# Padded score operands, zero matmuls in the prologue, a later tanh and a reordered end in a routed-attention and gated-FFN kernel

## The chip, the cores and the metric

The kernel runs on one core of a Trainium2 chip. The engines are named as the profile names them: PE (TensorE, the matmuls), PEld (its weight loads), DVE (VectorE), ACT (ScalarE), POOL (GpSimd) and SP (SyncE, which here only hands over DMAs). The metric is the device time of one execution in microseconds (us). The kernel before was run three times: 350.09 us in the median, from 348.97 to 357.59 us.

## The reference

Two blocks, one after the other. The first is attention in which a query sees only the keys of its own cluster; the second is an FFN with a convolution over the sequence (3 taps) and a gate.

```python
# attention: B=4, H=8, S=768, D=64, 16 clusters
q_assign = argmax(einsum('bhsd,hcd->bhsc', q_n, c_n))      # q, k, centroids normalised
k_assign = argmax(einsum('bhsd,hcd->bhsc', k_n, c_n))
mask   = q_assign[..., :, None] == k_assign[..., None, :]
scores = where(mask, q @ k.T / sqrt(D), -1e9)
attn   = softmax(scores);  x = attn @ v                     # heads side by side: 512 columns
# FFN: 512 -> 1024 -> 512
h    = maximum(x @ w_in, 0)
conv = sum over 3 taps of conv_w[k] * h shifted by k - 1 along S
out  = (h * sigmoid(conv)) @ w_out
```

## The kernel before, in words

**Attention.** There are 32 heads (4 batches of 8). For each head `load_qk` and `load_v` bring q, k and v in. `transposes` turns q and k (six 128x128 fp32 transposes on PE), `qkT_copy` takes them out of PSUM (DVE and ACT), `cast_qk` makes 16-bit copies on POOL and sends them by two DMAs into rows 0 to 63 of `extq` and `extk`. `assign` multiplies with the centroids (twelve fp32 matmuls of 32 columns), and `arg_a` and `arg_b` find each row's cluster (DVE and POOL) and make of it three more rows, which `bias_rows` transposes on PE (after POOL's last `pack` step) and sends by two more DMAs into rows 64 to 66. The rows make the masking part of the score matmul: 64 rows of data and 3 rows of cluster numbers give a score that is far below the others where clusters differ. `KC` is that 67.

**Slots.** The main loop has 32 slots `t`, each for two heads and one half (384) of the queries. A slot has six steps `scores(t, 0)` to `scores(t, 5)`: two matmuls (67 rows, 384 columns) into one of two PSUM buffers `sc`, then one exp on ACT. Between them the slot does, for the slot before it, `values` (attention times v, in three pairs of 12 matmuls), `normalize` (DVE: `rec`, then `x`), `x_transposes` and `xT_copy`.

**FFN units.** From slot 5 on a slot also does one unit `n = t - 5` of the FFN (256 of the 1024 hidden columns for half a sequence): `ffn_in(n, 0)` and `ffn_in(n, 1)` (four matmuls each, both into the PSUM bank `fp`), each followed by `relu` on ACT; then `taps(n, 0)` and `taps(n, 1)`, three DVE instructions each (the middle tap, L275, and the outer ones, L277). In the slot after that come `tanh` (ACT) and `gate` (DVE). In some slots `ffn_out` (eight matmuls of 512 columns into `fp`) and `evac` (a copy to SBUF and a DMA out) follow: 24 row blocks in all, `fouts` says in which slot; the ones that find no slot (`left`) are done at the end.

**Order.** Every engine works through its instructions in the order in which the program writes them; the order is written out by hand. `prepare(h, ...)` spreads the preparation of head `h` over places of the slots: three heads in slot 0, two in slot 1, one in each slot up to 25, none from 26 on. Nearly all DMAs go through SP's one queue, also in program order: loads, the two of `cast_qk`, the two of `bias_rows`, and the output. Slots 0 to 7 have no output and no or little FFN work; `half_slots_without_ffn` puts the loading of the weights there.

**Before the loop.** 24 fp32 transposes of the identity go to PE while the first loads run (L346); then heads 0, 1 and 2 are prepared in line.

**The end.** After slot 31 come unit 27 (`n` there), then units 28 to 31 (`last_in`), whose middle taps go to POOL; three whole row blocks of output; and for the last units `sigmoid`, `gate_sg` and the partial sums of the last four row blocks (`last_out`). ACT's order puts `tanh(27)` ahead of the relus of unit 28.

Of the kernel before, what the change touches and what calls it, by code (L numbers as in the profile page):

```python
# [8 lines left out]
F32 = mybir.dt.float32  # L9
# [8 lines left out]
def kernel(  # L18
# [31 lines left out]
    KC = D + 3  # L50
# [31 lines left out]
    oscale = const.tile([P, 1], F32, name="oscale")  # L82

# [82 lines left out]
    def bias_rows(h):  # L166
        pkT = where[h][1].bitcast(F16)[0 : 6 * J, 1024 - P : 1024]
        nc.tensor.transpose(pkT, pack_b[h % 3].rearrange("p a j -> p (a j)"), id16[:])  # L168
        spk = rot.tile([P, P], F16, name="spk", tag="spk")
        nc.vector.tensor_copy(out=spk[0 : 6 * J, :], in_=pkT)  # L170
        nc.sync.dma_start(extq_b[h % NE][D:KC, :], spk[0 : 3 * J, :])
        nc.sync.dma_start(extk_b[h % NE][D:KC, :], spk[3 * J : 6 * J, :])

# [6 lines left out]
    def scores(t, g):  # L180
        b, a, pr, h0 = slot(t)
        h = h0 + g // 3
        if g % 3 == 0:
            attn[t, g // 3] = rot.tile([P, J, HS], F16, name="attn", tag="attn", bufs=4)
        s = sc[nsc[0] % 2]
        nsc[0] += 1
        kt = 2 * (g % 3)
        for i in range(2):
            nc.tensor.matmul(  # L189
                s[:, i, 0:HS],  # L190
                lhsT=extk_b[h % NE][0:KC, P * (kt + i) : P * (kt + i + 1)],
                rhs=extq_b[h % NE][0:KC, HS * a : HS * (a + 1)],
                start=True,
                stop=True,
            )
        nc.scalar.activation(attn[t, g // 3][:, kt : kt + 2, :], s[:, :, 0:HS], AF.Exp, scale=0.125)  # L196
# [148 lines left out]
    for i in range(24):  # L345
        nc.tensor.transpose(sc[1][:, 0, 0:P], id128[:], id128[:])  # L346
# [22 lines left out]
    for i in range(NE):  # L369
        nc.gpsimd.memset(v16_b[i][:, :, D : D + 1], 1.0)  # L370

# [26 lines left out]
    def half_slots_without_ffn(t):  # L398
        if t == 0:
# [61 lines left out]
    for t in range(NT):  # L461
# [17 lines left out]
        if ng is not None:  # L479
            tanh(ng)  # L480
            gate(ng)
# [3 lines left out]
        if n is not None:  # L485
            if unit(n)[1]:
                carry(n)
            ffn_in(n, 0, fp)
            relu(n, 0, fp)
        run(t, 1)  # L490
        if vt is not None:
            values(vt, (2, 3))
# [22 lines left out]
        if fout:  # L515
            ffn_out(*fout, range(0, 4), fp)
        scores(t, 5)
        run(t, 5)
        if fout:
            ffn_out(*fout, range(4, NFB), fp)  # L520
            evac(*fout, fp, 0.5)
# [8 lines left out]
    ffn_in(n, 0, fp)  # L530
    relu(n, 0, fp)
# [3 lines left out]
    ffn_in(n, 1, fp)  # L535
    relu(n, 1, fp)
    carry(n)
# [5 lines left out]
    tanh(n)  # L543
    gate(n)
    left = [fouts.pop(t) for t in sorted(fouts)]
    whole = [x for x in left if x[0] < bl or x[1] < 2]

    def last_in(n):
        carry(n)
        for f, bank in enumerate((avb, fp)):  # L550
            ffn_in(n, f, bank)
            relu(n, f, bank)
            taps(n, f, nc.gpsimd)

    def last_out(u):
        for tq in range(2, J):
            ffn_out(bl, tq, (2 * u, 2 * u + 1), banks[tq - 2])
# [45 lines left out]
```

## Time and profile before

| what | value |
|---|---|
| median of 3 runs | 350.09 us (348.97 to 357.59) |
| profiled execution, time | 349.18 us |
| profiled execution, span | 347.4 us |
| mean granted PE clock | 0.919 of full |
| PE, DVE, ACT, POOL busy | 85%, 67%, 63%, 34% of the span |

The span is the time from the first instruction to the last of the profiled execution; its own device time is 1.8 us more. A row of the timeline gives the start, the time, the engine, the line, the operation and what it writes and reads, and in brackets how long the engine had been idle and whose end released it. A row of the chain of waits gives the start and the time of a piece of the path that ended last. PE is called busy while any matmul is under way, which is not the same as working at its best rate.

### The profile page before, as it was taken

To read this page: it belongs to the slowest core of one execution; us is meant where nothing else is said; L and a number is where in the kernel's file an instruction comes from. 1 tells how busy PE (TensorE), PEld (TensorE's weight loads), DVE (VectorE), ACT (ScalarE), POOL (GpSimd) and SP (SyncE) were. 2 spreads that over 40 slices of the span, in tenths; PEclk is the share of its full clock that TensorE was granted. 3 is DMA by queue.
4 is the path that set the end of the run, shared out by engine and by line. 5 is a ranking of instruction groups with operands and counts; after the bars stand their busy time and mean duration, and the time that the engine had idled before them with its cause. 6 is when DMAs were issued, how large, how long until landed. Compare 5 with 4: busy or idle time off the path is not lost.

```text
span 347.4 us, 7331 instructions
## 1 busy us (share of the span) xinstructions
PE 296.2 (85%) x2721; PEld 206.8 (60%) x2721; DVE 232.1 (67%) x512; ACT 217.8 (63%) x330; POOL 119.7 (34%) x276
## 2 busy tenths in 40 slices
PE   8799988997797998889999997899997877875863
PEld 7667767775565665566666665566664444542321
DVE  4542243437777788778888887788887776657682
ACT  4033335676677677667777786677777887862441
POOL 2254433644444233333333333333332000003460
PEclk9655557899989999999999999999999999998999
DMA  8386827673555146404444442344110000110203
GB/s 202 75 218 171 184 56 167 140 161 97 121 123 122 27 123 165 120 24 126 124 122 125 124 140 77 92 123 123 58 54 35 30 2 0 56 38 0 92 0 122
DMA packets 67194, 34.37 MB, mean 99 GB/s; under 512 B 53843, under 2 KB 64083, under 8 KB 67158
## 3 DMA queue, kind: packets, MB, share of 16 engines
q1 hardware_dynamic: 63286, 31.42, 33.1%
q0 software_dynamic: 2304, 2.10, 4.4%
q10 hardware_dynamic: 1568, 0.39, 0.5%
q8 instruction: 21, 0.34, 0.4%
q14 instruction: 15, 0.12, 0.1%
HBM read 23.11 MB, written 6.29 MB: 85 GB/s over the span
## 4 chain that ended last, share of the span: by engine, by line
DVE 41%; PE 40%; issue 8%; ACT 7%; POOL 2%; DVEq 0%; POOLq 0%; ACTq 0%
DVE cnv L277 18%; PE fp L245 10%; PE avb L203 8%; PE sc L189 6%; DVE cnv L275 6%; PE trb L134 6%; ACT attn L196 3%; DVE o_sb L326 3%; DVE eqq L148 3%; DVE x L216 3%; PE tra L110 2%; ACT th L293 2%; DVE mx L147 2%; DVE xT L230 2%; PE trb L168 2%
## 5 line engine op out<-in xcount | busy, mean ns | idle before, releaser
L196 ACT ACTIVATE attn<-sc 128x768 f16<-128x768 f32 x192 | 153.0, 809 | 82.6 <-PE sc L189 82.6
L189 PE MATMUL sc<-extq,extk 67*128 67x384 f16 x384 | 97.5, 342 | 6.9 <-ACT attn L196 6.9
L277 DVE SCALAR_TENSOR_TENSOR cnv<-hpad,cwcol,cnv 128x382 f16<-128x382 f16 (+1 forms) x128 | 80.7, 633 | 6.9 <-POOL cnv L275 2.7
L245 PE MATMUL fp<-xT,w_in 128*128 128x384 f16 x240 | 50.1, 331 | 8.6 <-DVE o_sb L326 5.1
L203 PEld LDWEIGHTS <-attn 128*128 128x128 f16 x1152 | 49.0, 100 | 8.4 <-issue 0.8
L203 PE MATMUL avb<-v,attn 128*128 128x65 f16 x1152 | 54.0, 197 | 0.0
L134 PEld LDWEIGHTS trb<-cT,qkT 128*128 128x128 f32 x360 | 50.2, 215 | 3.5 <-ACT qkT L116 1.3
L134 PE MATMUL trb<-cT,qkT 128*128 128x32 f32 x360 | 49.1, 291 | 0.1
L151 POOL TENSOR_TENSOR val<-eqq,iota_rev 128x192 f32<-128x192 f32 x30 | 17.7, 589 | 86.3 <-DVE eqq L148 86.3
L245 PEld LDWEIGHTS <-w_in 128*128 128x128 f16 x256 | 25.1, 99 | 34.2 <-issue 19.5
L189 PEld LDWEIGHTS <-extk 67*128 67x128 f16 x384 | 31.6, 103 | 20.6 <-issue 10.0
L121 POOL CAST c<-qkT 128x768 f16<-128x768 f32 x32 | 33.6, 1051 | 17.4 <-DVE qkT L115 9.4
L215 DVE RECIPROCAL rec<-avb 128x6 f32<-128x6 f32 x32 | 6.3, 196 | 45.2 <-PE avb L203 45.2
L312 PE MATMUL fp<-w_out,hg 128*128 128x512 f16 x136 | 34.9, 378 | 0.0
L312 PEld LDWEIGHTS <-hg 128*128 128x128 f16 x192 | 18.5, 98 | 25.3 <-DVE hg L308 6.3
L256 ACT ACTIVATE hpad<-fp 128x384 f16<-128x384 f32 x60 | 29.4, 490 | 5.2 <-PE fp L245 5.1
L297 DVE SCALAR_TENSOR_TENSOR hg<-th,hpad 128x764 f16<-128x764 f32 (+1 forms) x28 | 26.7, 954 | 5.8 <-ACT th L293 5.3
L293 ACT ACTIVATE th<-cnv 128x764 f32<-128x764 f16 (+1 forms) x28 | 23.6, 842 | 8.0 <-DVE cnv L277 8.0
L275 DVE TENSOR_SCALAR cnv<-hpad,cwcol 128x382 f16<-128x382 f16 (+1 forms) x56 | 23.8, 425 | 0.0
L115 DVE COPY qkT<-tra 128x512 f32<-128x512 f32 x30 | 20.5, 684 | 4.4 <-PE tra L110 4.4
L147 DVE TENSOR_REDUCE mx<-trb 128x12 f32<-128x192 f32 x30 | 10.6, 353 | 18.1 <-PE trb L134 18.1
L110 PE MATMUL tra<-id,qk_in 128*128 128x128 f32 x120 | 22.1, 315 | 0.0
(100 smaller groups left out, 286.6 us busy)
## 6 DMA issues: line engine op xcount, KB each, us to landing
qk_in<-in_q_dram SPq DMA_DIRECT2D x32, 192.0 KB
v_in<-in_v_dram SPq DMA_DIRECT2D x32, 192.0 KB
out_dram<-o_sb SPq DMA_DIRECT2D x24, 256.0 KB
qk_in<-in_k_dram SPq DMA_DIRECT2D x30, 192.0 KB
extq<-c SPq DMA_DIRECT2D x32, 96.0 KB
extk<-c SPq DMA_DIRECT2D x32, 96.0 KB
w_in<-in_moe_w_in_dram POOLq DMA_DIRECT2D x8, 128.0 KB, 4.4
w_out<-in_moe_w_out_dram POOLq DMA_DIRECT2D x8, 128.0 KB, 3.1
```

Of the source, the lines that this page charges most:

```text
L110: nc.tensor.transpose(to, qk_t[h][:, j].rearrange("p a d -> p (a d)"), id128[:])
L121: nc.gpsimd.tensor_copy(out=c[:], in_=qkT[h][:])
L134: nc.tensor.matmul(tb[:, 256 + 32 * j : 288 + 32 * j], lhsT=qkT[h][:, P * j : P * (j + 1)], rhs=cT32[:, h % H, :], start=True, stop=True,)
L189: nc.tensor.matmul(s[:, i, 0:HS], lhsT=extk_b[h % NE][0:KC, P * (kt + i) : P * (kt + i + 1)], rhs=extq_b[h % NE][0:KC, HS * a : HS * (a + 1)],
L196: nc.scalar.activation(attn[t, g // 3][:, kt : kt + 2, :], s[:, :, 0:HS], AF.Exp, scale=0.125)
L203: nc.tensor.matmul(avp[:, u, 0 : D + 1], lhsT=attn[t, hd][:, kt, P * jq : P * (jq + 1)], rhs=v16_b[(h0 + hd) % NE][:, kt, 0 : D + 1], star ...
L245: nc.tensor.matmul(bank[:, 0:HS], lhsT=w_in16[:, r, 2 * u + f, :], rhs=xT[:, b % 2, r, HS * a : HS * (a + 1)], start=(r == 0), stop=(r == ...
L256: nc.scalar.activation(hpad(n)[:, f, o : o + HS], bank[:, 0:HS], AF.Relu)
L275: (eng or nc.vector).tensor_scalar(out=cnv, in0=src, scalar1=w, scalar2=None, op0=ALU.mult)
L277: nc.vector.scalar_tensor_tensor(out=cnv, in0=src, scalar=w, in1=cnv, op0=ALU.mult, op1=ALU.add)
L293: nc.scalar.activation(th_t[n][:, :, 0:N], cnv_t.pop(n)[:, :, 0:N], AF.Tanh, scale=0.5)
L312: nc.tensor.matmul(bank[:, 0:Dm], lhsT=hg_b[b][:, fb, P * tq : P * (tq + 1)], rhs=w_out16[:, fb, :], start=(fb == 0), stop=(fb == NFB - 1) ...
```

## The change

- `extq` and `extk` are used with all 128 rows in the score matmuls. Rows 64 to 127 are set to zero once per buffer by `ext_rows`: for buffers 0 to 3 on POOL ahead of head 0, for 4 to 11 at the end of slots 0, 1 and 2, `extq` by DVE and `extk` by POOL. `bias_rows` still writes rows 64 to 66.
- `keep_busy(n)` issues `n` matmuls of a 16-bit identity with 512 columns of zeros into `sc[1]`. Twelve of them take the place of the 24 transposes; 2, 5, 6 and 6 more stand between the steps that prepare heads 0 to 2.
- In a slot, `tanh` moves from ahead of `scores(t, 1)` to behind `relu(n, 0)`, and `gate` behind the steps of place 1. The `evac` of a slot goes to ACT instead of DVE.
- Unit 27's two `ffn_in` and `relu` move into slot 31, into the bank `trb`.
- At the end the middle taps of units 28 to 31 go to ACT (a copy with a scale) instead of POOL; the banks alternate between `avb`/`fp` and `tra`/`trb`; `last_in(28)` stands ahead of `gate(27)`; the three whole row blocks get a bank each, and only one of them is evacuated on ACT.

```diff
-    KC = D + 3
+    BR = 3
+    zero = const.tile([P, 512], F16, name="zero")
 # scores
-                lhsT=extk_b[h % NE][0:KC, P * (kt + i) : P * (kt + i + 1)],
-                rhs=extq_b[h % NE][0:KC, HS * a : HS * (a + 1)],
+                lhsT=extk_b[h % NE][:, P * (kt + i) : P * (kt + i + 1)],
+                rhs=extq_b[h % NE][:, HS * a : HS * (a + 1)],
 # ahead of the loop
-    for i in range(24):
-        nc.tensor.transpose(sc[1][:, 0, 0:P], id128[:], id128[:])
+    nc.vector.memset(zero.bitcast(F32)[:], 0.0)
+    def keep_busy(n):
+        for i in range(n):
+            nc.tensor.matmul(sc[1][:, i % 2, :], lhsT=id16[:], rhs=zero[:], start=True, stop=True)
+    keep_busy(12)
...
-    for i in range(NE):
+    def ext_rows(i, eng=nc.gpsimd):
+        eng.memset(extq_b[i].bitcast(F32)[D:P, :], 0.0)
+        nc.gpsimd.memset(extk_b[i].bitcast(F32)[D:P, :], 0.0)
         nc.gpsimd.memset(v16_b[i][:, :, D : D + 1], 1.0)
+    for i in range(4):
+        ext_rows(i)
...
     cast_qk(0)
+    keep_busy(2)
     qkT_copy(1)
...
     assign(1)
+    keep_busy(5)
     bias_rows(0)
...
     transposes(2, (avb[:], fp[:]))
+    keep_busy(6)
     qkT_copy(2)
     bias_rows(1)
     assign(2)
+    keep_busy(6)
     cast_qk(2)
...
     def half_slots_without_ffn(t):
+        for i in ((4, 5, 6, 7), (8, 9), (10, 11))[t] if t < 3 else ():
+            ext_rows(i, nc.vector)
 # in a slot
         run(t, 0)
-        if ng is not None:
-            tanh(ng)
-            gate(ng)
...
             relu(n, 0, fp)
+        if ng is not None:
+            tanh(ng)
         run(t, 1)
+        if ng is not None:
+            gate(ng)
...
             x_transposes(vt)
+        if t == NT - 1:
+            ffn_in(n + 1, 0, trb)
+            relu(n + 1, 0, trb)
         scores(t, 4)
...
             ffn_out(*fout, range(0, 4), fp)
+        if t == NT - 1:
+            ffn_in(n + 1, 1, trb)
+            relu(n + 1, 1, trb)
+            carry(n + 1)
         scores(t, 5)
...
-            evac(*fout, fp, 0.5)
+            evac(*fout, fp, 0.5, on_act=True)
 # the end
+    def last_in(n):
+        carry(n)
+        for f in range(2):
+            bank = ((avb, fp), (tra, trb))[n % 2][f]
+            ffn_in(n, f, bank)
+            relu(n, f, bank)
+        for f in range(2):
+            w = cwcol[:, 2 * unit(n)[2] + f, 1:2]
+            ...
+            nc.scalar.activation(cnv_t[n][:, f, :], hpad(n)[:, f, 2 : 2 + S - CUT], AF.Copy, scale=w)
+            tap(n, f, 0)
+            tap(n, f, 2)
     tanh(n - 1)
     values(NT - 1, range(J))
     normalize(NT - 1)
-    ffn_in(n, 1, fp)
-    relu(n, 1, fp)
-    carry(n)
     gate(n - 1)
...
     taps(n, 0)
     taps(n, 1)
     tanh(n)
+    last_in(n0)
     gate(n)
-    last_in(n0)
     last_in(n0 + 1)
     for i, (b, tq) in enumerate(whole):
-        bank = (tra, trb)[i % 2]
+        bank = banks[i]
         ffn_out(b, tq, range(NFB), bank)
-        evac(b, tq, bank, 0.5, on_act=(i % 2 == 0))
+        evac(b, tq, bank, 0.5, on_act=(i == 1))
```

More of the change, by code (lines that the diff above doesn't have):

```diff
@@ L170, in bias_rows @@
         nc.vector.tensor_copy(out=spk[0 : 6 * J, :], in_=pkT)
-        nc.sync.dma_start(extq_b[h % NE][D:KC, :], spk[0 : 3 * J, :])
-        nc.sync.dma_start(extk_b[h % NE][D:KC, :], spk[3 * J : 6 * J, :])
+        nc.sync.dma_start(extq_b[h % NE][D : D + BR, :], spk[0 : 3 * J, :])
+        nc.sync.dma_start(extk_b[h % NE][D : D + BR, :], spk[3 * J : 6 * J, :])
     nsc = [0]
@@ L529, with last_out @@
     banks = [sc[0][:, 0, :], sc[0][:, 1, :], sc[1][:, 0, :], sc[1][:, 1, :]]
-    ffn_in(n, 0, fp)
-    relu(n, 0, fp)
+    left = [fouts.pop(t) for t in sorted(fouts)]
+    whole = [x for x in left if x[0] < bl or x[1] < 2]
+    def last_in(n):
[6 more added lines that the diff above has]
+            w = cwcol[:, 2 * unit(n)[2] + f, 1:2]
+            if n not in cnv_t:
+                cnv_t[n] = rot.tile([P, 2, S - CUT], F16, name="cnv", tag="cnv")
+            nc.scalar.activation(cnv_t[n][:, f, :], hpad(n)[:, f, 2 : 2 + S - CUT], AF.Copy, scale=w)
+            tap(n, f, 0)
+            tap(n, f, 2)
+    def last_out(u):
+        for tq in range(2, J):
+            ffn_out(bl, tq, (2 * u, 2 * u + 1), banks[tq - 2])
     tanh(n - 1)
@@ L543 @@
     tanh(n)
+    last_in(n0)
     gate(n)
[L545 to L557, printed above, removed]
-    last_in(n0)
     last_in(n0 + 1)
     for i, (b, tq) in enumerate(whole):
-        bank = (tra, trb)[i % 2]
+        bank = banks[i]
         ffn_out(b, tq, range(NFB), bank)
-        evac(b, tq, bank, 0.5, on_act=(i % 2 == 0))
+        evac(b, tq, bank, 0.5, on_act=(i == 1))
     for u in range(NPR):
```

## The prediction

> **What bounds the kernel now.** I read the page first, for the clock granted to PE over the span; then the engines' busy time in stretches; then the timeline of the first 75 us; then the chain of waits and the timeline of single slots; last the end. The page's row of PE's clock (40 slices of 8.7 us) has a hole of some 40 us:
>
> ```profile
> PEclk9655557899989999999999999999999999998999
> ```
>
> Asked in fine steps, the clock changes only at times that lie a multiple of 3.41 us apart, so I cut the busy table on that grid. Columns: stretch, length, busy us (instructions) of PE, PEld, DVE, ACT, POOL, then clock, DMA share, GB/s.
>
> ```profile
> 42.15:45.56 3.41, 3.41 (x25) 3.04 (x25) 1.96 (x6) 0.81 (x1) 0.84 (x3) 0.50 0.67 153
> 52.39:55.81 3.42, 3.28 (x29) 2.77 (x30) 0.91 (x2) 0.56 (x2) 2.16 (x5) 0.50 0.57 86
> ...
> 62.64:66.05 3.41, 3.41 (x42) 2.87 (x39) 1.73 (x5) 2.51 (x4) 1.61 (x3) 1.00 0.72 134
> 66.05:69.46 3.41, 3.41 (x23) 2.39 (x22) 1.13 (x3) 1.86 (x4) 2.63 (x7) 0.50 0.61 149
> 83.12:86.53 3.41, 1.88 (x22) 1.07 (x20) 2.26 (x5) 2.04 (x4) 2.59 (x6) 1.00 0.16 56
> ```
>
> PE was busy for all of 62.64 to 66.05 and lost the clock at its end; in 83.12 to 86.53 it was busy for 1.88 of 3.41 us and kept it; in 42.15 to 45.56 it was wholly busy and did not get it back. So it isn't busy time that holds the clock. The large groups of matmuls in the stretch that lost it (first two rows) and in the one that kept it (next two), and four score matmuls in the chain of waits:
>
> ```profile
> L189 PE MATMUL sc<-extq,extk 67*128 67x384 f16 x7 | 1.8, 343 | 0.0
> L134 PE MATMUL trb<-cT,qkT 128*128 128x32 f32 x12 | 1.4, 269 | 0.0
> ...
> L245 PE MATMUL fp<-xT,w_in 128*128 128x384 f16 x6 | 1.3, 325 | 0.0
> L189 PE MATMUL sc<-extq,extk 67*128 67x384 f16 x3 | 0.8, 324 | 0.0
> ...
> 64.76 0.65 PE sc L189 x4
> ```
>
> Four score matmuls in a row take 0.65 us, so 384 columns stream for 0.16 us. These matmuls stream 7 x 0.16 = 1.1 us in the losing stretch and 9 x 0.16 = 1.4 us in the keeping one; weighted by used rows (67 of 128 for scores) it is 0.6 against 1.2 us. I take it that the share of the array that streams is what counts; two stretches make that likely, not certain.
>
> **Up to slot 5.** The first score matmuls of slots 0 to 5, and three other rows of that time:
>
> ```profile
> 17.25 0.83 PE L189 MATMUL sc<-extq,extk 67*128 67x384 f16 x2
> ...
> 34.54 0.83 PE L189 MATMUL sc<-extq,extk 67*128 67x384 f16 x2
> ...
> 50.71 0.80 PE L189 MATMUL sc<-extq,extk 67*128 67x384 f16 x2
> ...
> 59.80 0.48 PE L189 MATMUL sc<-extq,extk 67*128 67x384 f16 x2 [0.57 <-ACT attn L196]
> ...
> 65.98 0.77 PE L189 MATMUL sc<-extq,extk 67*128 67x384 f16 x2
> ...
> 73.73 0.49 PE L189 MATMUL sc<-extq,extk 67*128 67x384 f16 x2 [0.57 <-ACT attn L196]
> ```
>
> ```profile
> 16.67 0.53 SPq L122 DMA_DIRECT2D extq<-c  x1
> ...
> 23.56 0.91 PEld L110 LDWEIGHTS tra<-id,qk_in 128*128 128x128 f32 x4 [0.23 <-DMA qk_in<-in_k_dram]
> ...
> 30.35 0.75 SPq L172 DMA_DIRECT2D extk<-spk  x1
> ```
>
> Slots 0 to 4 take 17.3, 16.2, 9.1, 6.2 and 7.8 us. Slots 0 and 1 run at half clock and prepare three and two heads; slots 2 and 4 run at half in part; slot 3 is wholly at full clock.
>
> Slot 0 can't shrink by half. From 16.67 to 31.1 us SP hands over 20 DMAs one right behind another (first and last shown), and the change removes none. The last are the cluster rows of head 2, with which slot 1 starts, so it can't start before about 32. PE also has to wait for head 4's keys, which come at 23.5, with slot 0 half done; that wait may well cost the clock for a stretch or two. I put slot 1 at 33 instead of 34.5: gain 1.5.
>
> Slot 1 is PE work throughout, 16.2 us at half clock, so 8 at full; 10 with waits for `pack`, and 11.5 with a stretch or two at half: gain 4.7. The padding decides here: it makes two score steps and one head's transposes stream about as much as the 52.39 stretch did, at whose end the clock came back. Slot 2 takes 6.7, slot 3's 6.2 and some memsets: gain 2.4. In slot 4 the dip of the 66.05 row goes: gain 1.5. Sum 10.1.
>
> What this costs:
>
> ```profile
> 323.59 1.47 PE trb L312 x7
> ...
> L341 DVE MEMSET cT<- 128x256 f32 x1 | 0.3, 272 | 0.9 <-PEq L587 0.9
> ...
> 7.36 0.82 POOL L121 CAST c<-qkT 128x768 f16<-128x768 f32 x1 [4.86 <-DVE qkT L115]
> ```
>
> A matmul of 512 columns streams 1.47 / 7 = 0.21 us, 0.42 at half clock. The first twelve cost 2.5 to 5 us beside loads that are awaited anyway. The other 19 cost 4.0 us; I let them delay slot 0 by nothing, since `assign(2)` runs in half its time and the rest lies in PE's waits for `pack`. Were the clock at half all the same, they would be 8.1, and some 4 would stick out. A memset of 64x384 is an estimated 0.4 us (256 columns took 0.27 on DVE; no row shows this fill on POOL, where I allow 0.2 to 1). Eight on POOL are 3.4 us, inside the 4.86 for which it idles ahead of its first cast. Those at the ends of slots 0 to 2 put 1 us on the path. The 61 more rows cost PE nothing: with 67 rows and with 128 a matmul of 384 columns shows 324 and 325 ns above. So up to slot 5 the gain is 9 us, between 2 (clock as before) and 13.
>
> [...]
>
> **The slots from 5 on.** Behind a slot with output (chain of waits, then two rows of the timeline, then two groups of the page):
>
> ```profile
> 159.97 0.21 DVE rec L215
> ...
> 165.31 0.61 DVE o_sb L326
> ...
> 165.96 0.81 PE fp L245 x4
> ...
> 168.81 0.21 DVE rec L215
> ```
>
> ```profile
> 165.27 0.49 PE L189 MATMUL sc<-extq,extk 67*128 67x384 f16 x2
> ...
> 166.00 0.21 POOL L164 TENSOR_TENSOR pack<-pack,kscale 128x12 f16<-128x12 f16 x1
> ```
>
> ```profile
> L256 ACT ACTIVATE hpad<-fp 128x384 f16<-128x384 f32 x60 | 29.4, 490 | 5.2 <-PE fp L245 5.1
> L297 DVE SCALAR_TENSOR_TENSOR hg<-th,hpad 128x764 f16<-128x764 f32 (+1 forms) x28 | 26.7, 954 | 5.8 <-ACT th L293 5.3
> ```
>
> The period is 168.81 - 159.97 = 8.84. PE has one hole: two score matmuls from 165.27 stream until 165.60, and `ffn_in` starts at 165.96, when DVE has emptied `fp`. With the copy on ACT, right behind the last `ffn_out`, this 0.36 goes, and PE alone would make 8.48. Late next is a loop: from `rec` to the end of DVE's preparation steps 5.34 (159.97 to 165.31), POOL's `pack` 0.9 (to 166.21), and bias rows to `rec` 2.04 (166.77 to 168.81): 8.3. And the gate now stands in front of `rec`: `ffn_in` 0.81, relu 0.49, tanh 0.85 and gate 0.95 end 3.1 us behind the start of `ffn_in`, the values 2.85 (168.81 - 165.96). It sticks out by 0.25, of which PE's slack takes half. Period 8.6, gain 0.24 in each of 13 slots (those behind slots 9, 10, 13 to 18, 21 to 25): 3.1.
>
> Behind a slot without output:
>
> ```profile
> 137.84 0.85 ACT th L293
> ...
> 147.05 0.85 ACT th L293
> ```
>
> ```profile
> 138.84 0.91 POOL L164 TENSOR_TENSOR pack<-pack,kscale 128x12 f16<-128x12 f16 x1
> ```
>
> The period is 9.21. Tanh waits for the last tap and holds up an exp and a relu; the gate behind it then runs beside POOL's `pack`, which takes 0.91 instead of 0.21. With both later that 0.7 goes and 8.5 is left: gain 0.7 in 8 slots (behind 5 to 8, 11, 12, 19, 20), 5.6.
>
> From slot 27 on no head is prepared, and the wait behind tanh is plain:
>
> ```profile
> 281.34 0.81 PE L245 MATMUL fp<-xT,w_in 128*128 128x384 f16 x4 [1.19 <-ACT hpad L256]
> ```
>
> These 1.19 us go; the wait for `x` and the gate in front of `rec` take half of it back: 0.55 in five slots, 2.8. Together 11.5, between 1 (the gate's 0.95 all ahead of `rec`) and 14.
>
> **The end.**
>
> ```profile
> 318.83 1.44 PE L245 MATMUL avb<-xT,w_in 128*128 128x384 f16 x4 [3.41 <-ACT hpad L256]
> ...
> 330.37 2.49 POOL L275 TENSOR_SCALAR cnv<-hpad,cwcol 128x386 f16<-128x386 f16 x2 [4.86 <-issue]
> ```
>
> Unit 27's eight matmuls in slot 31 spare the last values a wait for `fp`; I count 0.75. A unit's two middle taps took POOL 2.49; two ACT copies are 2 x 0.49 (the relu's row; no row has a copy of this shape), so 1.5 less for each unit that waits for them, three of the four: 4.5. Against that `gate(27)` now stands behind taps that wait for ACT's tanh, two relus and a copy, 0.85 + 3 x 0.49 = 2.3, with 1.6 on the path, as PE waited there before too (3.41). Gain 3.5 (0 to 5).
>
> **The rivals.**
> 1. Rows and zeros don't count, and the clock stays as it was. For it: PE's long busy stretches at half clock had score matmuls in them as well. Against: the groups above. The prologue gains 2 instead of 9, or loses 2 if the 19 zero matmuls run at half: 333 to 338.
> 2. The gate takes the place of the tanh: it stands whole in front of `rec`, and the slots gain nothing. For it: DVE is in the loop in every slot. Against: by the sum above only 0.25 of its 0.95 sticks out. 337; with the first, 345.
> 3. Slower: ACT becomes the bound of the slots. Per slot with output it has 6 exps, 2 relus, tanh, part of `qkT` and now the evacuation; if 0.85 (tanh) in 27 slots came ahead of exps that PE awaits and nothing else got shorter, 23 us less the 12.5 of prologue and end, 360. It decides from where ACT has under 0.85 us of idling left in a slot. Against: ACT waited for PE ahead of its exps for 82.6 us in all:
>
> ```profile
> L196 ACT ACTIVATE attn<-sc 128x768 f16<-128x768 f32 x192 | 153.0, 809 | 82.6 <-PE sc L189 82.6
> ```
>
> **How the numbers follow.** The profiled execution took 349.18 us (span 347.4). Less 9, 11.5 and 3.5 it is 325.2; the median of the runs stands 0.9 above it: 326. Forecast 0.62; rival 1 alone 0.17; rival 2 alone 0.12; both 0.05; rival 3 0.04. The forecast's own range is 317 to 335 (prologue 13 or 4, slots 14 or 8, end 5 or 2). To hold 8 in 10 it takes in rivals 1 and 2 as well: 316 to 340. A change of 2%, 7 us, is about what can be told from none here: below 343 lie the forecast and the first two, 0.88 with something off for sums that are wrong together; within 2% 0.08; slower 0.04.
>
> **What would show it.** The clock row: full through 11 to 21 us, a dip where PE waits for head 4's keys, full again by 40 at the latest; no dip near 66 and 100. Slot 1 starts at 32 to 34, slot 5 at 62 to 68. The periods fall to about 8.6 and 8.5; PE's wait for `fp` is gone, POOL's `pack` is at 0.21 in all slots. DVE's wait ahead of `rec` is near nil, with the gate right before it. In the last 30 us POOL has no taps. I am wrong if the clock stays at half in slot 1, if the period stays over 8.8, or if slot 0 starts later than 18.5.

## The result, and the profile after

The changed kernel takes 336.35 us in the median of 4 runs (335.39 to 337.16); its time is 0.962 of the kernel before (95% interval 0.958 to 0.966). The forecast was 326 us with a range of 316 to 340: faster, as forecast, but between the profiled executions only 13.2 us of the 24 came. Disturbed executions are left out of all comparisons here; the profile of one experiment (67 rows) is of a disturbed execution, so only its times are used. The profiled execution took 335.94 us, its span is 334.2 us.

The page's row of PE's clock, of the changed kernel (40 slices of 8.35 us):

```profile
PEclk9985876999999999999999999999999999997699
```

The dips that the kernel before had near 66 and 100 us are gone. Two things are not as forecast: between 22 and 56 us the clock is at 0.50 in three stretches (22.2 to 32.5, 39.3 to 46.1 and 49.5 to 56.4), and again for 10 us near the end (305.5 to 315.8). The starts of slots 0 to 5 and 31 in the timeline show what this cost:

```profile
17.94 0.49 PE L190 MATMUL sc<-extq,extk 128*128 128x384 f16 x2
...
33.79 0.49 PE L190 MATMUL sc<-extq,extk 128*128 128x384 f16 x2
...
48.69 0.48 PE L190 MATMUL sc<-extq,extk 128*128 128x384 f16 x2
...
58.96 0.32 PE L190 MATMUL sc<-extq,extk 128*128 128x384 f16 x1 [0.57 <-ACT attn L197]
...
71.29 0.48 PE L190 MATMUL sc<-extq,extk 128*128 128x384 f16 x2 [0.57 <-DMA qk_in<-in_k_dram]
...
286.77 0.49 PE L190 MATMUL sc<-extq,extk 128*128 128x384 f16 x2
```

| part | before, us | after, us | gain | forecast |
|---|---|---|---|---|
| up to the start of slot 5 | 73.7 | 71.3 | 2.4 | 9 (2 to 13) |
| from slot 5 to the start of slot 31 | 227.5 | 215.5 | 12.0 | 11.5 (1 to 14) |
| from there to the end of the span | 46.2 | 47.4 | -1.2 | 3.5 (0 to 5) |

**The slots came out.** Two neighbouring slots with output in the changed kernel, from the timeline:

```profile
161.33 0.19 DVE L216 RECIPROCAL rec<-avb 128x6 f32<-128x6 f32 x1
...
165.38 0.60 ACT L325 ACTIVATE o_sb<-fp 128x512 f32<-128x512 f32 x1
...
166.86 0.81 PE L246 MATMUL fp<-xT,w_in 128*128 128x384 f16 x4
167.36 0.21 POOL L165 TENSOR_TENSOR pack<-pack,kscale 128x12 f16<-128x12 f16 x1
...
169.02 0.95 DVE L298 SCALAR_TENSOR_TENSOR hg<-th,hpad 128x764 f16<-128x764 f32 x1 [0.92 <-ACT th L294]
...
169.89 0.19 DVE L216 RECIPROCAL rec<-avb 128x6 f32<-128x6 f32 x1
```

From `rec` to `rec` it is 8.56 (forecast 8.6). `ffn_in` no longer waits for `fp`, `pack` takes 0.21, and the gate stands right before `rec`, which then waits for nothing: each as forecast. DVE's wait has moved ahead of the gate, 0.92 us for tanh.

**Slot 1 did not.** DVE in slot 1 of the changed kernel, and three stretches on the clock's grid (columns as in the prediction):

```profile
35.51 0.35 DVE L160 TENSOR_REDUCE m_t<-val 128x12 f32<-128x192 f32 x1 [0.70 <-POOL val L152]
36.00 1.60 DVE L377 MEMSET extq<- 64x384 f32 x4
37.63 0.22 DVE L171 COPY spk<-trb 36x128 f16<-36x128 f16 x1
```

```profile
29.04:32.45 3.41, 3.14 (x14) 1.72 (x13) 1.98 (x5) 1.19 (x2) 1.25 (x4) 0.50 0.71 199
...
35.87:39.28 3.41, 1.39 (x21) 1.27 (x21) 2.48 (x7) 1.08 (x2) 2.69 (x10) 1.00 0.80 196
39.28:42.69 3.41, 3.41 (x26) 3.14 (x24) 0.42 (x2) 0.92 (x2) 3.08 (x14) 0.50 0.94 218
```

The clock came back at 32.45, ahead of slot 1. Then four memsets of `extq` held DVE for 1.6 us; the copy `spk` stood behind them and PE's next bias rows behind `spk`. PE was busy for 1.39 of 3.41 us, and the clock was gone again for 6.83 us.

**The end got longer.** DVE, PE and ACT behind the loop of the changed kernel:

```profile
304.23 2.46 DVE L278 SCALAR_TENSOR_TENSOR cnv<-hpad,cwcol,cnv 128x386 f16<-128x386 f16 x4 [2.23 <-ACT cnv L569]
306.61 0.94 DVE L298 SCALAR_TENSOR_TENSOR hg<-th,hpad 128x764 f16<-128x764 f32 x1
...
309.85 0.69 DVE L327 TENSOR_SCALAR o_sb<-sc 128x512 f32<-128x512 f32 x1
...
310.59 6.15 PE L313 MATMUL sc<-w_out,hg 128*128 128x512 f16 x16 [7.61 <-DVE o_sb L327]
...
314.19 0.60 ACT L325 ACTIVATE o_sb<-sc 128x512 f32<-128x512 f32 x1 [7.73 <-PE sc L313]
```

PE does the first whole row block, then waits 7.61 us for DVE's copy of it: the copy stands behind the taps of units 28 and 29 and the gate, and the second block's bank lies in the same PSUM tile. In this wait the clock falls to 0.50, and the next 16 matmuls take 6.15 us (3.62 at full clock in the combined kernel below). ACT's copy of the second block, and behind it the first `sigmoid`, wait for those.

### The profile page after: what moved, and what is told of

It reads as the page before. It is cut to its first block, busy times and chain, and to the rows that moved or that the text cites. A ratio compares the mean times of both kernels' runs of the same rounds, so it can differ in the third digit from the quotient of the medians.

```text
span 334.2 us, 7350 instructions
## 1 busy us (share of the span) xinstructions
PE 286.8 (86%) x2728; PEld 197.6 (59%) x2728; DVE 226.3 (68%) x505; ACT 227.6 (68%) x354; POOL 105.8 (32%) x284
## 4 chain that ended last, share of the span: by engine, by line
PE 57%; DVE 22%; ACT 9%; issue 4%; DMA 3%; POOL 2%; SPq 2%; POOLq 0%; DVEq 0%; ACTq 0%
PE sc L190 12%; PE trb L135 8%; PE fp L313 8%; PE avb L204 8%; DVE cnv L278 7%; PE fp L246 6%; ACT attn L197 4%; PE tra L111 4%; PE sc L313 3%; DVE hg L298 3%; DMA qk_in<-in_k_dram 3%; DVE x L217 3%; ACT th L294 2%; DVE cnv L276 2%; PE sc L350 2%
## 5 line engine op out<-in xcount | busy, mean ns | idle before, releaser
L190 PE MATMUL sc<-extq,extk 128*128 128x384 f16 x384 | 94.4, 334 | 6.9 <-ACT attn L197 6.3
L278 DVE SCALAR_TENSOR_TENSOR cnv<-hpad,cwcol,cnv 128x382 f16<-128x382 f16 (+1 forms) x128 | 78.9, 619 | 7.9 <-ACT cnv L569 3.6
L204 PEld LDWEIGHTS <-attn 128*128 128x128 f16 x1152 | 48.2, 99 | 8.8 <-issue 1.4
L135 PEld LDWEIGHTS trb<-cT,qkT 128*128 128x128 f32 x360 | 46.7, 202 | 3.8 <-ACT qkT L117 1.9
L135 PE MATMUL trb<-cT,qkT 128*128 128x32 f32 x360 | 45.7, 279 | 0.2 <-DVE qkT L116 0.2
L246 PE MATMUL fp<-xT,w_in 128*128 128x384 f16 x224 | 45.5, 326 | 0.3
L190 PEld LDWEIGHTS <-extk 128*128 128x128 f16 x384 | 30.7, 100 | 21.0 <-issue 10.4
L152 POOL TENSOR_TENSOR val<-eqq,iota_rev 128x192 f32<-128x192 f32 x30 | 17.7, 590 | 77.7 <-DVE eqq L149 77.7
L246 PEld LDWEIGHTS <-w_in 128*128 128x128 f16 x256 | 24.8, 97 | 18.3 <-issue 1.9
L313 PE MATMUL fp<-w_out,hg 128*128 128x512 f16 x136 | 34.9, 379 | 0.0
L122 POOL CAST c<-qkT 128x768 f16<-128x768 f32 x32 | 26.9, 841 | 10.0 <-DVE spk L171 5.2
L257 ACT ACTIVATE hpad<-fp 128x384 f16<-128x384 f32 x56 | 27.7, 495 | 0.2 <-PE fp L246 0.2
L313 PE MATMUL sc<-w_out,hg 128*128 128x512 f16 x56 | 15.5, 434 | 9.8 <-DVE o_sb L327 7.6
L127 POOL CAST v<-v_in 128x384 f16<-128x384 f32 x32 | 20.6, 645 | 1.5 <-DMA v_in<-in_v_dram 1.5
```

The costliest lines, as they stand in the source:

```text
L135: nc.tensor.matmul(tb[:, 256 + 32 * j : 288 + 32 * j], lhsT=qkT[h][:, P * j : P * (j + 1)], rhs=cT32[:, h % H, :], start=True, stop=True,)
L190: nc.tensor.matmul(s[:, i, 0:HS], lhsT=extk_b[h % NE][:, P * (kt + i) : P * (kt + i + 1)], rhs=extq_b[h % NE][:, HS * a : HS * (a + 1)], s ...
L204: nc.tensor.matmul(avp[:, u, 0 : D + 1], lhsT=attn[t, hd][:, kt, P * jq : P * (jq + 1)], rhs=v16_b[(h0 + hd) % NE][:, kt, 0 : D + 1], star ...
L246: nc.tensor.matmul(bank[:, 0:HS], lhsT=w_in16[:, r, 2 * u + f, :], rhs=xT[:, b % 2, r, HS * a : HS * (a + 1)], start=(r == 0), stop=(r == ...
L257: nc.scalar.activation(hpad(n)[:, f, o : o + HS], bank[:, 0:HS], AF.Relu)
L278: nc.vector.scalar_tensor_tensor(out=cnv, in0=src, scalar=w, in1=cnv, op0=ALU.mult, op1=ALU.add)
```

## The experiments

The theory after the result: (a) the padding lets PE keep its clock, as forecast, but the memsets on DVE in slot 1 (and perhaps the matmuls on zeros) give most of it back; (b) the slots' gain comes from the later tanh and from the evacuation on ACT as forecast; (c) the new end loses by its order and its banks. The rivals stand with each run. All stages come from one profiled execution per kernel; times are medians, for two kernels the values themselves. Each ratio is to the kernel before as it was run beside that kernel. Kernels with the same slots differ by up to 0.7 us in the part from slot 5 to slot 31 (215.5 to 216.2).

| kernel | time | ratio to before (95%) | slot 0 | slot 5 | 5 to 31 | 31 to end |
|---|---|---|---|---|---|---|
| before | 350.09 | 1 | 17.3 | 73.7 | 227.5 | 46.2 |
| changed | 336.35 | 0.962 (0.958, 0.966) | 17.9 | 71.3 | 215.5 | 47.4 |
| slots' edits alone | 336.5 and 338.7 | 0.963 (0.955, 0.971) | 17.6 | 74.2 | 216.7 | 43.8 |
| 67 rows | 342.1 to 345.2 | 0.977 (0.970, 0.985) | | | | |
| memsets early | 334.85 | 0.955 (0.950, 0.960) | 18.1 | 69.5 | 216.1 | 46.9 |
| other banks | 336.13 | 0.958 (0.952, 0.964) | 19.0 | 73.8 | 216.1 | 45.1 |
| old end | 336.37 | 0.960 (0.956, 0.965) | 18.3 | 72.7 | 216.1 | 45.5 |
| no zeros in line | 337.1 | 0.964 (0.958, 0.969) | 18.2 | 72.3 | 215.6 | 47.4 |
| more zeros | 334.68 | 0.955 (0.947, 0.963) | 19.0 | 71.7 | 216.2 | 46.7 |
| gate first | 335.61 | 0.959 (0.953, 0.965) | 18.8 | 73.7 | 215.6 | 46.6 |
| combined | 330.93 | 0.944 (0.938, 0.950) | 20.2 | 68.2 | 216.2 | 44.2 |
| padding alone | 343.84 | 0.981 (0.973, 0.989) | 17.7 | 65.8 | 227.4 | 47.1 |
| evacuation on DVE | 341.05 | 0.978 (0.967, 0.989) | 17.9 | 69.0 | 221.6 | 47.2 |
| tanh at its old place | 345.61 | 0.985 (0.978, 0.992) | 18.6 | 70.4 | 226.1 | 47.2 |

### The slots: each edit alone

The kernel before with the slots' edits and nothing else:

```diff
         run(t, 0)
-        if ng is not None:
-            tanh(ng)
-            gate(ng)
...
             relu(n, 0, fp)
+        if ng is not None:
+            tanh(ng)
         run(t, 1)
+        if ng is not None:
+            gate(ng)
...
-            evac(*fout, fp, 0.5)
+            evac(*fout, fp, 0.5, on_act=True)
```

> The kernel before with the three edits inside a slot alone: tanh behind relu(n, 0), gate behind place 1, the slot's evacuation on ACT. My theory: these edits alone make the gain that the changed kernel shows between slot 5 and slot 31 (227.5 us before, 215.5 after), so 12 us, about 338 us in all, with the slots up to 5 and the end as before (73.7 us to the start of slot 5; 46 us from the start of slot 31). Rival: part of those 12 us comes from the padded scores (more rows, a steadier clock); then slots 5 to 31 come out at 218 us or more and the time at 340.5 or more.

Measured: 216.7 us from slot 5 to slot 31 instead of 227.5, so these edits alone bring 10.8 of the 12.0. The dips of the clock near 67 and 91 us stayed; this kernel's score matmuls still use 67 rows. The profiled executions of this kernel and of the whole change are 0.5 us apart in span: what the rest of the change gains and loses beside the slots' edits nearly cancels.

Each of the two undone in the changed kernel:

```diff
-            evac(*fout, fp, 0.5, on_act=True)
+            evac(*fout, fp, 0.5)
```

> The changed kernel with the evacuation in the slots back on DVE. Theory, as forecast: it is worth 0.24 to 0.36 us in each slot with output, by the wait of PE for fp; periods behind such slots 8.75 to 8.85, the others 8.5 as in the changed kernel; from slot 5 to 31 218.5 to 220 instead of 215.5; time 339 to 341. Rival: the later tanh and gate bring all of it, and PE's wait for fp is covered; 215.5 to 216 and 336.5.

```diff
         run(t, 0)
+        if ng is not None:
+            tanh(ng)
+            gate(ng)
...
-        if ng is not None:
-            tanh(ng)
         run(t, 1)
-        if ng is not None:
-            gate(ng)
```

> The changed kernel with tanh and gate back at their old place, ahead of the slot's first values; the evacuation stays on ACT. Theory, as forecast: the later tanh and gate are worth 0.7 us in each slot without output and 0.55 in each of the last five slots, and little in the slots with output; periods 9.2 and 8.6, from slot 5 to 31 222 to 224 instead of 215.5, time 342.5 to 344.5. Rival 1: with the evacuation gone from DVE the old place costs little; 217 to 219, time 338 to 340. Rival 2: the old place costs in every slot, because ACT now has tanh and evacuation ahead of exps; 226 or more, time 347.

From slot 5 to slot 31 it takes:

| | tanh at its old place | tanh later |
|---|---|---|
| evacuation on DVE | 227.4 | 221.6 |
| evacuation on ACT | 226.1 | 215.5 |

Alone the evacuation is worth 1.3 us and the later tanh 5.8; together 11.9. The starts of slots 15 and 16 with what lies between them; first with the evacuation on DVE, with the wait ahead of `ffn_in` in the second row, then with tanh at its old place, with the gate and POOL's cast beside it:

```profile
155.53 0.33 PE L190 MATMUL sc<-extq,extk 128*128 128x384 f16 x1
...
157.72 0.81 PE L246 MATMUL fp<-xT,w_in 128*128 128x384 f16 x4 [0.34 <-DVE o_sb L327]
...
164.49 0.33 PE L190 MATMUL sc<-extq,extk 128*128 128x384 f16 x1
```

```profile
160.33 0.33 PE L190 MATMUL sc<-extq,extk 128*128 128x384 f16 x1
...
162.86 1.36 DVE L298 SCALAR_TENSOR_TENSOR hg<-th,hpad 128x764 f16<-128x764 f32 x1 [0.53 <-ACT th L294]
...
163.36 1.23 POOL L127 CAST v<-v_in 128x384 f16<-128x384 f32 x1
163.40 0.51 ACT L257 ACTIVATE hpad<-fp 128x384 f16<-128x384 f32 x1
163.96 0.81 PE L246 MATMUL fp<-xT,w_in 128*128 128x384 f16 x4 [0.17 <-ACT hpad L257]
...
169.11 0.33 PE L190 MATMUL sc<-extq,extk 128*128 128x384 f16 x1
```

The periods are 8.96 and 8.78, against 8.84 with neither edit and 8.55 with both. With the later tanh alone, a slot with output even gets longer than before: the gate ahead of `rec` delays what follows on DVE, the evacuation stands at the end of that, and PE waits 0.34 us for `fp`. With the evacuation on ACT alone, tanh still pushes the relu back and PE waits for that. That both waits have to go before either edit pays in full is how I read these rows; no run removes one wait by itself. The theory for the evacuation (218.5 to 220) was low, and for tanh the second rival's number came (226), though not for its reason: PE's scores wait no longer for ACT's exps than in the changed kernel (6.3 us in both pages), and the gain of each edit hangs on the other.

### The first slots: rows, memsets, zeros

The changed kernel with the score matmuls back at 67 rows; the memsets stay:

```diff
-                lhsT=extk_b[h % NE][:, P * (kt + i) : P * (kt + i + 1)],
-                rhs=extq_b[h % NE][:, HS * a : HS * (a + 1)],
+                lhsT=extk_b[h % NE][0 : D + BR, P * (kt + i) : P * (kt + i + 1)],
+                rhs=extq_b[h % NE][0 : D + BR, HS * a : HS * (a + 1)],
```

> The changed kernel with 67 instead of 128 rows in the score matmuls; the memsets, the zero matmuls and the rest stay. Theory that the clock follows the streamed share weighted by rows: PE loses the clock again near 66 and 100 us and gets it back later in slots 1 and 2, so slot 5 starts 2 to 4 us later (73 to 75 instead of 71.3) and the time is 338.5 to 341. Rival, rows don't count: the clock row and the start of slot 5 stay within 0.7 us of the changed kernel, and so does the time (336.4).

It loses 6 to 9 us, more than either expected. The granted clock over the span is 0.914 to 0.921 in these runs, against 0.947 to 0.955 in those of the changed kernel. The rival that rows don't count falls.

The memsets of buffers 4 to 7 go to POOL behind `cast_v(0)`, those of 8 to 11 to POOL alone:

```diff
     cast_v(0)
+    for i in (4, 5, 6, 7):
+        ext_rows(i)
...
-        for i in ((4, 5, 6, 7), (8, 9), (10, 11))[t] if t < 3 else ():
-            ext_rows(i, nc.vector)
+        for i in ((), (8, 9), (10, 11))[t] if t < 3 else ():
+            ext_rows(i)
```

> The changed kernel with the zero rows of buffers 4 to 7 written on POOL ahead of the loop, behind cast_v(0), where POOL idles for 5.2 us, and those of 8 to 11 on POOL alone instead of DVE and POOL. Theory: the memsets in DVE's queue at the end of slot 0 make PE wait 2.0 us for the bias rows of head 5, and that idle stretch costs the clock for the next two windows (39.3 to 46.1). Without them PE keeps the clock in slot 1, and slot 2 starts 4 to 6 us earlier (43 to 45 instead of 48.7); time 330 to 333. Rival, SP's queue and the loads set slots 1 and 2 anyway: slot 2 starts within 1.5 us of 48.7 and the time stays above 335.

The median is 1.5 us lower, less than the theory, and the ranges of the two kernels overlap (333.59 to 335.77, and 335.39 to 337.16). DVE's memsets are gone from slot 1, but in this execution the clock had not come back at slot 1's start; it stayed at half from 22.4 to 46.3 us. So this run doesn't show what the memsets cost when the clock is back. The next one comes nearer to it: the kernel before with only the rows padded and the memsets for them, at these early places on POOL.

```diff
-                lhsT=extk_b[h % NE][0:KC, P * (kt + i) : P * (kt + i + 1)],
-                rhs=extq_b[h % NE][0:KC, HS * a : HS * (a + 1)],
+                lhsT=extk_b[h % NE][:, P * (kt + i) : P * (kt + i + 1)],
+                rhs=extq_b[h % NE][:, HS * a : HS * (a + 1)],
...
+    for i in range(4):
+        ext_rows(i)
...
     cast_v(0)
+    for i in (4, 5, 6, 7):
+        ext_rows(i)
```

> The kernel before with nothing but the score operands at 128 rows and the memsets for them (all on POOL, buffers 4 to 7 early); the 24 transposes, the order of the slots and the end stay. Theory: the rows act on the clock alone; the first stretch at half ends near 46 instead of 56, the dips near 66 and 100 are gone, slot 5 starts at 71 to 72.5 instead of 73.7, the slots from 5 to 31 take 226 to 227.5 as before, and the time is 346 to 348.5. Rival 1: the rows do nothing by themselves; clock and time as before, 349 to 351. Rival 2: the run with 67 rows in the changed kernel lost 6 to 9 us, so the rows are worth that much here too: 341 to 344.

Slot 5 comes at 65.8, earlier than any theory had it, and the time, 343.84, is the second rival's. The page's clock row, the starts of slots 1, 2 and 5, and three stretches on the grid, all of this kernel:

```profile
PEclk9755999999999999999999999999999999996999
```

```profile
33.97 0.33 PE L189 MATMUL sc<-extq,extk 128*128 128x384 f16 x1
...
45.87 0.32 PE L189 MATMUL sc<-extq,extk 128*128 128x384 f16 x1
...
65.82 0.48 PE L189 MATMUL sc<-extq,extk 128*128 128x384 f16 x2 [0.57 <-ACT attn L196]
```

```profile
29.22:32.63 3.41, 3.14 (x14) 1.72 (x13) 1.98 (x5) 1.20 (x2) 1.26 (x5) 0.50 0.41 127
...
36.04:39.46 3.42, 2.41 (x29) 1.99 (x28) 1.03 (x4) 1.80 (x3) 2.94 (x14) 1.00 0.88 216
...
46.28:49.70 3.42, 2.08 (x35) 1.79 (x35) 1.26 (x3) 1.42 (x3) 2.65 (x8) 1.00 0.27 65
```

Slot 1 starts as in the changed kernel (33.97 and 33.79), with the clock back at 32.63 and 32.45: a pair alike up to there. PE's wait ahead of the second bias rows in slot 1, first in the changed kernel, then in this one:

```profile
37.90 0.21 PE L169 MATMUL trb<-id,pack 128*36 128x128 f16 x1 [2.02 <-DVE spk L171]
```

```profile
37.08 0.23 PE L168 MATMUL trb<-id,pack 128*36 128x128 f16 x1 [1.01 <-POOL oscale L410]
```

Without memsets on DVE slot 1 then takes 11.90 us instead of 14.90, the clock stays, and slot 5 comes 5.5 us sooner. This is one execution of each, and the pair differs in the matmuls on zeros as well, so the 5.5 is not a price that the memsets have everywhere. The six profiled kernels with the changed kernel's code up to slot 5 start that slot at 69.0 to 73.8; with the early memsets beside the same zeros it is 69.5, and 68.2 in the combined kernel below. In that one, without memsets on DVE, PE waited 1.29 us for a DMA of bias rows at the start of slot 1, and the clock went at 34.9 all the same.

It is also the plainest evidence for the rows: beside the memsets only they differ from the kernel before, whose clock came back at 55.8 and went twice more before 309; here it comes at 32.6 and stays to 309, through stretches in which PE is busy for 2.08 and 2.41 of 3.41 us. The slots behind slot 5 are unchanged (227.4), and a score matmul there shows the same time with 67 and with 128 rows. The groups of the score matmuls from 150 to 200 us, of the kernel before and of this one:

```profile
L189 PE MATMUL sc<-extq,extk 67*128 67x384 f16 x69 | 17.0, 325 | 0.0
```

```profile
L189 PE MATMUL sc<-extq,extk 128*128 128x384 f16 x70 | 16.9, 325 | 0.6 <-ACT attn L196 0.6
```

The changed kernel without the 19 matmuls on zeros between the first heads' steps (the first 12 stay):

```diff
-    keep_busy(2)
-    keep_busy(5)
-    keep_busy(6)
-    keep_busy(6)
```

> The changed kernel without the 19 matmuls on zeros that stand between the first heads' steps (the first 12 on zeros, ahead of the centroids' transpose, stay). Theory: they hold the clock at full from 11 to 22 us and buy little else, because the clock falls at 22 in any case; without them the clock falls at 12, slot 0 starts at 17.9 or a little later (18.5), slot 1 at 34 to 35, and the time is 336 to 338. Rival 1: they cost PE more than they give; slot 0 starts 0.7 earlier, at 17.2, and the time is 335 or less. Rival 2: they carry the whole gain of the first slots; slot 5 comes at 73.5 as in the kernel before, and the time is 338.5.

As the theory had it: the clock falls at 13.1 us (and comes back at 26.7), and the time is 337.1, too near the 336.35 to call it a difference. The 19 matmuls hold the clock for some 9 us more and buy nothing that shows.

The changed kernel with early memsets and 38 more matmuls on zeros in PE's waits:

```diff
+    def fill(cnt):
+        for i in range(cnt):
+            nc.tensor.matmul(fp[:], lhsT=id16[:], rhs=zero[:], start=True, stop=True)
+    for t, place, cnt in ((0, 2, 8), (0, 4, 6), (1, 0, 8), (1, 2, 4), (1, 5, 4), (2, 0, 8)):
+        at(t, place, lambda cnt=cnt: fill(cnt))
```

> The changed kernel with the memsets of buffers 4 to 7 early on POOL (as in the run of that name) and 38 more matmuls on zeros, in slot 0 ahead of head 4's transposes (8) and head 5's (6), in slot 1 at its start (8), in its third (4) and last part (4), and at the start of slot 2 (8), all into fp, which nothing reads then. Theory: PE's waits in slots 0 and 1 let the clock fall and the clock sets their length; with the waits filled the clock stays full from 5 to 60, slot 1 starts at 32.5 to 33.5 (SP's queue sets that) and takes 11 to 12 instead of 14.9, slot 5 starts at 65 to 67 instead of 71.3, and the time is 330 to 332. Rival: the slots are set by loads and by the chains through POOL and DVE to the bias rows, not by the clock; the clock is full, but slot 5 starts at 69 to 71 and the time is 334 to 336. A third way: the zeros stand in PE's queue ahead of needed matmuls and slot 5 comes later than 71.3.

The time is that of the run with early memsets alone (334.7 and 334.9), as the first rival had it, but slot 5 comes at 71.7, as the third way had it. Slots 1 and 2 and the wait in slot 0, from its timeline:

```profile
26.16 0.66 PE L111 MATMUL tra<-id,qk_in 128*128 128x128 f32 x4 [1.63 <-DMA qk_in<-in_k_dram]
...
37.10 0.49 PE L190 MATMUL sc<-extq,extk 128*128 128x384 f16 x2
...
51.24 0.68 PE L190 MATMUL sc<-extq,extk 128*128 128x384 f16 x2
```

The clock was at full in slot 1 (from 34.6 to 48.2), and slot 1 still took 14.1 us. The fills in it cost PE 1.89, 1.03 and 1.91 us of its own queue (the last at half clock); it seems that they took what the clock gave. Slot 0 was not helped: head 4's keys came 1.63 us after the eight fills ended.

### The end

The changed kernel with the whole end of the kernel before (unit 27 behind the loop, middle taps on POOL, banks `tra` and `trb`):

```diff
-        if t == NT - 1:
-            ffn_in(n + 1, 0, trb)
-            relu(n + 1, 0, trb)
...
-            nc.scalar.activation(cnv_t[n][:, f, :], hpad(n)[:, f, 2 : 2 + S - CUT], AF.Copy, scale=w)
-            tap(n, f, 0)
-            tap(n, f, 2)
+            taps(n, f, nc.gpsimd)
...
-        bank = banks[i]
+        bank = (tra, trb)[i % 2]
```

> The changed kernel with the end of the kernel before (unit 27's first matmuls behind the loop, the middle taps of units 28 to 31 on POOL, whole output blocks in the banks of tra and trb, gate of unit 27 ahead of unit 28). Theory: the new end is a loss of its own; from the start of slot 31 to the end the changed kernel takes 47.4 us, and the kernel before with nothing but the slots' edits 43.8, so this kernel should take 43.8 there: slot 31 at 286.8 as in the changed kernel, span 330.6, time 332.3, ratio 0.950. Rival: the 43.8 was the luck of where the clock fell in one profiled execution; then the end takes 46 to 47.5 and the time is 335 to 336.5.

The theory's 3.6 us fell: the end takes 45.5 and the time is 336.37, that of the changed kernel. The same old end takes 43.8, 46.2, 45.5 and 47.1 us in the four kernels of the table that have it, with 0, 3.4, 3.4 and 6.8 us of half clock in its middle; so the lowest of them goes with a clock that was not lost there. The new end takes 46.6 to 47.4 in seven kernels that have it as it is or with the gate moved, always with 6.8 or 10.2 us of half clock. Its loss is about 1.5 us on the profiles, and no difference in the times shows it. This run puts all edits of the end back at once, so it doesn't tell them apart.

The whole row blocks in banks of two tiles in turn:

```diff
-        bank = banks[i]
+        bank = (banks[0], banks[2], banks[1])[i]
```

> The changed kernel with one edit at the end: the second whole row block goes into the first half of sc[1] and the third into the second half of sc[0], instead of the other way round. Theory: the second block waited for the evacuation of the first (to 310.6) only because both lie in the tile sc[0]; in another tile it starts when gate(27) ends, at about 307.6, and the clock comes back 3.4 us earlier: 3 to 4.5 us less, 332 to 333.5. Rival, it waited for something else that ends then, such as the taps of unit 29 in front of it on DVE: it still starts at 310.6, and the time stays within 0.7 us.

PE then runs straight on to the block that needs unit 27:

```profile
304.18 3.19 PE L313 MATMUL sc<-w_out,hg 128*128 128x512 f16 x14
...
309.70 0.95 DVE L298 SCALAR_TENSOR_TENSOR hg<-th,hpad 128x764 f16<-128x764 f32 x1
...
310.70 0.70 PE L313 MATMUL sc<-w_out,hg 128*128 128x512 f16 x2 [3.34 <-DVE hg L298]
```

and waits for its gate. The end takes 45.1 instead of 47.4. The median of the times (336.13) is no lower; in the profiled execution slot 5 came 2.5 us later, and the other executions have no profile. The gate of unit 27 ahead of the taps of unit 28:

```diff
     tanh(n)
-    last_in(n0)
     gate(n)
+    last_in(n0)
```

> The changed kernel with the gate of unit 27 ahead of the taps of unit 28 on DVE, as before the change. Theory: in the changed kernel that gate stands behind four taps that wait 2.23 us for ACT's middle taps, and the last blocks wait for it; moved ahead, it ends about 3 us sooner, and the end from slot 31's start takes 45 to 46 instead of 47.4: time 334.5 to 335. Rival: the order doesn't matter, because the second matrix product of the output blocks waits for its bank until the first one is evacuated (7.61 us of waiting were put down to that); the end stays at 47 to 47.5 and the time at 336.

Here the gate is early, and the wait for the first block's copy stays:

```profile
306.71 4.84 DVE L278 SCALAR_TENSOR_TENSOR cnv<-hpad,cwcol,cnv 128x386 f16<-128x386 f16 x8 [0.31 <-ACT cnv L569]
...
311.46 0.69 DVE L327 TENSOR_SCALAR o_sb<-sc 128x512 f32<-128x512 f32 x1
...
312.20 6.23 PE L313 MATMUL sc<-w_out,hg 128*128 128x512 f16 x16 [6.74 <-DVE o_sb L327]
```

The end takes 46.6, a gain of 0.8. Each of the two uncovers the other's wait, so the last run has both, with the early memsets:

```diff
     cast_v(0)
+    for i in (4, 5, 6, 7):
+        ext_rows(i)
...
-        for i in ((4, 5, 6, 7), (8, 9), (10, 11))[t] if t < 3 else ():
-            ext_rows(i, nc.vector)
+        for i in ((), (8, 9), (10, 11))[t] if t < 3 else ():
+            ext_rows(i)
...
-        bank = banks[i]
+        bank = (banks[0], banks[2], banks[1])[i]
...
-    last_in(n0)
     gate(n)
+    last_in(n0)
```

> The changed kernel with three things together: the memsets of buffers 4 to 11 on POOL (4 to 7 early), the whole output blocks in banks of two different tiles in turn, and the gate of unit 27 ahead of the taps of unit 28. Theory: at the end PE first waits for the evacuation of the first block, which stands on DVE behind taps, since the second block's bank is in the same tile, and with other banks it waits for the gate of unit 27; each of the two alone uncovers the other, so both together gain more than the 2.3 and 0.8 us that they gained alone: from slot 31's start 43 to 44 instead of 47.4, with no or one stretch at half clock near 305 to 318. With slot 5 at 69.5 to 71 and 216 from there to slot 31 the time is 330 to 333. Rival: what is late at the end is the chain of units 28 to 31 on ACT and DVE; the end stays at 45 and the time at 333 to 335.

```profile
298.63 3.62 PE L313 MATMUL sc<-w_out,hg 128*128 128x512 f16 x16
...
300.50 0.95 DVE L298 SCALAR_TENSOR_TENSOR hg<-th,hpad 128x764 f16<-128x764 f32 x1 [0.97 <-ACT th L294]
...
307.26 3.57 PE L313 MATMUL sc<-w_out,hg 128*128 128x512 f16 x8 [5.02 <-DVE o_sb L327]
```

The first two blocks now run straight on, 16 matmuls in 3.62 us at full clock. The third still waits 5.02 us for a copy that stands behind taps on DVE, in which the clock goes, for 6.8 us. The end takes 44.2, so 3.2 less than 47.4. That is about the sum of the 2.3 and 0.8 alone; that both together gain more, as the theory had it, isn't shown. The time is 330.93 (330.11 to 331.73), and this kernel beats the one before and the changed one.

## Why the prediction was right, and where it failed

**The slots (11.5 forecast, 12.0 measured).** Right in sum and in its marks. The terms were mis-sized: the 13 slots with output gained 4.9 us in all and not 3.1, those without 4.1 and not 5.6, the last five 3.0 (2.8). The step "the gate now stands in front of `rec`" was right. What the gate costs there by itself isn't measured: with the evacuation left on DVE the period is 8.96, 0.12 longer than with neither edit, and with both edits it is 8.55, near the 8.48 that PE alone was said to make. Rival 2 falls, as the gate's place costs nothing that shows with both edits in. Rival 3 falls too: the scores of the changed kernel wait no longer for ACT's exps than before (6.3 and 6.9 us), as its page shows:

```profile
L190 PE MATMUL sc<-extq,extk 128*128 128x384 f16 x384 | 94.4, 334 | 6.9 <-ACT attn L197 6.3
```

**The first slots (9 forecast, 2.4 measured).** That the rows move the clock was right. Padding alone brings slot 1 to 34.0 and makes it 11.9 us long (33 and 11.5 forecast), without dips near 66 and 100, and slot 5 falls into the 62 to 68 named; the gain is 7.9. The step that failed is "those at the ends of slots 0 to 2 put 1 us on the path". The four memsets cost DVE 1.60, near the estimated 0.4 each; but they stand ahead of `spk` when PE has nothing else, PE's wait there is 2.02 instead of 1.01 us, and in the matched pair the clock went with it: 3.0 us in slot 1 and 5.5 up to slot 5. A price was put on the memsets' length and none on the clock that hangs on them. How much of the missing 6.6 us they explain stays open, since moving them in the changed kernel itself brought 1.5. "I am wrong if the clock stays at half in slot 1": it was so for half of it. Of the zeros, the claim that they delay slot 0 by nothing was not far off (17.9 for 17.3, and 18.2 without those in line), but they were counted as a help, and no run shows them to be one. Whether they are the reason that slot 5 comes at 68 to 70 with early memsets and zeros, and at 65.8 with early memsets alone, stays open: the grid's position differed between those executions too (a point of it lies at 32.63 us with the padding alone, at 32.69 with the memsets early and at 34.9 in the combined kernel).

**Rival 1** (rows don't count) falls by two runs: 67 rows cost 6 to 9 us, padding alone gives 343.84. PE's busy time by itself doesn't tell the stretches apart either: with the padding alone the clock stayed behind those with 2.41 and 2.08 of 3.41 us busy, and in the changed kernel it was gone behind two with more, as its grid shows:

```profile
18.80:22.21 3.41, 2.62 (x20) 1.76 (x18) 1.54 (x4) 1.88 (x4) 1.66 (x5) 1.00 0.84 223
22.21:25.63 3.42, 1.20 (x6) 1.21 (x7) 0.49 (x3) 0.40 (x1) 1.92 (x6) 0.50 0.89 223
...
46.11:49.52 3.41, 2.48 (x18) 1.61 (x17) 1.30 (x5) 1.93 (x3) 1.18 (x3) 1.00 0.24 58
49.52:52.93 3.41, 2.42 (x20) 2.19 (x21) 1.67 (x4) 0.88 (x2) 2.89 (x10) 0.50 0.31 71
```

The share that streams, which the prediction took from two stretches, was the author's estimate. The runs show that the rows count; what share the clock needs was not shown.

**The end (3.5 forecast, -1.2 measured, outside its own bounds).** Two steps failed. "1.5 less for each unit that waits", 4.5 in all, was too large. DVE's outer taps of the last units waited 2.7 us in all for POOL's middle taps before, and 3.6 us for ACT's in the changed kernel, as the groups by form show:

```profile
L277 DVE SCALAR_TENSOR_TENSOR cnv<-hpad,cwcol,cnv 128x386 f16<-128x386 f16 x64 | 41.2, 649 | 4.7 <-POOL cnv L275 2.7
```

```profile
L278 DVE SCALAR_TENSOR_TENSOR cnv<-hpad,cwcol,cnv 128x386 f16<-128x386 f16 x64 | 39.4, 621 | 5.6 <-ACT cnv L569 3.6
```

No run moves the middle taps alone. And the sum left out an edit of the diff: the whole blocks moved into banks of `sc` and the first copy from ACT to DVE. That copy stands behind eight taps, and the wait of 7.61 us comes from there. It isn't all of the lost clock: with other banks the half clock there still lasts 6.8 us instead of 10.2. The wait of the gate behind ACT-fed taps was seen (1.6), and alone it is worth 0.8.

## What to carry to other kernels

Where an engine's granted clock falls in its waits, as PE's fell to 0.50 here behind a stretch with 1.39 of 3.41 us busy, price a delay also by the clock that the waiting engine can lose, and not by its length alone: in the one matched pair here, 1.6 us of memsets in a queue went with 5.5 us. Fixed work such as memsets belongs where the engine waits anyway. Matmuls on zeros moved the clock here (it fell at 22.2 us with the 19 in line and at 13.1 without), and no run shows that they saved time. When two edits relieve the same loop, measure them as a two by two table: here 1.3 and 5.8 alone made 11.9 together.

## What the runs showed of the hardware that was not expected

With 128 rows the clock survived stretches in which PE is busy for 2.08 and 2.41 of 3.41 us (padding alone), and it went behind ones with 1.39, 2.48 and 2.62 (changed kernel); with 67 rows it went behind one of 3.41 and stayed behind one of 1.88 (kernel before). So 61 more rows of zeros cost a score matmul no time (325 ns with 67 rows and with 128) and help to hold the clock (over the span 0.947 to 0.955 in the changed kernel, 0.914 to 0.921 with 67 rows in it). The gate on DVE takes 0.95 us alone and 1.36 beside POOL's cast of v, which takes 1.23 then and 0.51 otherwise. Beside POOL's cast of q and k in the kernel before, the gate stays at 0.95, and that cast takes 1.42 instead of 0.82. The runs don't show what the two share.
